# Hyena gate after duo attention on one core: the inverse transform of two batches split into a cosine and a sine part

## The chip, the core and the metric

The kernel runs on one core of a Trainium2 chip. The time is that of the device, in microseconds (us), from the first to the last instruction of one execution. PE is the matrix engine (TensorE), DVE the vector engine, ACT the scalar engine, POOL the GpSimd engine and SP the engine whose queue issues most of the DMAs.

## What is computed

Attention for 4 batches of 8 heads with 768 tokens of 64 numbers is followed by a gated long convolution. Four heads are causal over all keys ("R"); four see 4 sink tokens and a window of 64 ("L"). Cut to what matters here:

```python
a = softmax(where(mask, q @ k.T / 8, -1e9))      # per batch and head
x = (a @ v)                                      # put together to (4, 768, 512)
x1, x2, x3 = split(x @ w_proj, 3)                # 512 -> 3 * 512
X2 = rfft(x2, n=768, axis=1)
H  = rfft(filter_fft, n=768, axis=0)
conv = irfft(X2 * H, n=768, axis=1)
out = (x1 * conv * x3) @ w_out
```

The inverse transform `irfft` of the last two of the four batches is what changes.

## The kernel before

The work is a list of some 990 small named operations. The string `FAST` fixes in which order they are written, and with that the order on every engine: `name/engine@slot`, where `/v`, `/s`, `/p` and `/d` put an operation on DVE, ACT, POOL or a DMA of SP, and the slot is one of four places of two PSUM banks. A matmul group whose slot still holds an unread result waits for the reader. No scheduler changes this order afterwards.

Attention runs over n = 0 to 15, which are pairs of heads (batch n // 4). Pair n has `cqk` (cast of q and k), `T` (transposes them, from n = 8 by DMA on SP's queue), `sc` (scores, PE), `ex` (exp, ACT), `mk` (mask, DVE), `at` (values, PE), `rec` and `nm` (normalise, DVE), `fd`, `fe`, `fA`, `fS`, `fb`, `fr` (folds ahead of the forward transform, DVE or POOL), `W` (forward transform over tokens, PE), and `tn` (transposed attention for the projection). `lv15` loads v of the last pair, and `cv15` casts it.

The gate runs over the batches b = 0 to 3:

- `X` (24 matmuls of 512 columns for each batch) projects the transformed tokens, `Xe` evicts the result, and `pa`, `pb`, `pc` multiply it with the filter's spectrum: the tile `P` with three thirds. `sw` swaps two halves of one third by DMA.
- `x1` and `x3` are the projections for the gate, in blocks cb = 0 to 3 of 128 channels and halves of 384 tokens; `xs` evicts `x1`, and `g` multiplies with `x3` from PSUM.
- `c{b}.{cb}.{r}` (L1190) is the inverse transform. The 768 tokens are two halves, token t and token t + 384. r = 0 and r = 1 are the sums over even and odd frequencies; each takes three matmuls of 384 columns, with a third of `P` as the weights and a tile of the table `Gi` as the moving operand. `ce` (fp32 copy to `evs`, which lies in the tile `angle`) and `cv{b}.{cb}.0` and `.1` (L1201, DVE, sum and difference, written to `conv`, which lies in `turns`) turn the two into the two halves.
- `y` multiplies `conv` into the gate (for cb = 3: with `x1s`, and `g` then comes last), and `o{b}.{i}.{part}` (L1225) is the output projection of 128 tokens: part 0 takes the blocks cb = 0 to 2, part 1 the block cb = 3. `oe` evicts and `st` stores. For b = 3 tile i = 5 is done in two halves of 256 columns (L1220).

At the end of the program b = 3 is alone with what is left of b = 2: its `c`, `cv`, `y` and `g` end in `o3.*`, the evictions and the stores.

The lines that the prediction's steps touch most are these:

```python
SPECTRUM = (((0, 0), (0, 1)), ((1, 0), (1, 1)), ((0, 2), (1, 2)))
INVERSE = (((1, 0, 3), (1, 1, 4), (2, 1, 5)), ((0, 0, 0), (0, 1, 1), (2, 0, 2)))
```

An entry of `INVERSE` names a third of `P`, its half and a tile of `Gi`: r = 0 needs the second third and one half of the last, r = 1 the first third and the other half of the last. Tiles 3 and 0 are cosines, 4 and 1 sines, and 5 and 2 hold cosines in rows 0 to 63 and sines in rows 64 to 127.

## Time and profile before

| what | value |
|---|---|
| time, median of 3 runs (lowest to highest) | 185.48 us (185.42 to 185.55) |
| profiled execution: span, its only time on record | 186.0 us |
| mean granted TensorE clock | 0.993 |
| matmuls of L1190 (inverse transform, all batches) | 96 of 384 columns |
| DMA | 33.44 MB, mean 180 GB/s |

The span lies 0.5 us above the median of the runs. A row of the profile's timeline gives the start and the length of a group of instructions, then engine, line, operation, output and input tiles, shapes and count. Matmuls overlap in the records, so the length of one matmul (0.33 us for 384 columns) is longer than the distance from one to the next; a row of x12 matmuls in the chain of work gives that distance when it is divided by 12.

### The profile page before, as it was taken

The numbers are of one execution on the slowest core, as the hardware profiler recorded it, in microseconds if no ns is written. First come the engines' busy times: TensorE is split into PE (matmuls) and PEld (weight loads), VectorE is DVE, ScalarE is ACT, GpSimd is POOL, SyncE is SP. The second block draws the span as 40 slices with busy tenths as digits, with TensorE's granted clock in tenths as the row PEclk, the third lists the DMA queues.
The fourth block names the chain that finished last, engine by engine and source line by source line (L and its number), as shares of the span: only waits on it lengthen the run. The fifth ranks groups of instructions, "written<-read, shape, count | busy, mean of one in ns | idle before, by whom it ended". The sixth has DMA issues, their size and how long they took to land.

```text
span 186.0 us, 4370 instructions
## 1 busy us (share of the span) xinstructions
PE 171.6 (92%) x1685; PEld 102.2 (55%) x1702; DVE 152.5 (82%) x297; ACT 142.2 (76%) x186; POOL 83.5 (45%) x99
## 2 busy tenths in 40 slices
...
GB/s 163 305 305 194 257 272 244 260 215 130 211 224 217 104 217 222 177 149 221 216 239 201 223 203 171 127 252 222 124 102 40 118 0 131 40 4 113 188 281 108
DMA packets 76836, 33.44 MB, mean 180 GB/s; under 512 B 66058, under 2 KB 73226, under 8 KB 76810
## 3 DMA queue, kind: packets, MB, share of 16 engines
...
q8 instruction: 14, 0.23, 0.6%
...
q14 instruction: 12, 0.10, 0.1%
...
## 4 chain that ended last, share of the span: by engine, by line
PE 65%; DMA 16%; ACT 4%; DVE 4%; SPq 3%; POOL 3%; issue 2%; POOLq 0%
PE f_x_ps L1160 20%; PE f_out_ps L1225 10%; PE f_X_ps L1125 10%; DMA f_filt<-in_moe_filter_fft_dram 7%; PE f_c_ps L1190 7%; PE f_sc L961 6%; PE f_att L1021 4%; DMA f_qkT<-f_qk_bf 4%; DMA f_v_f<-in_v_dram 3%; SPq L898 3%; DMA qk_ahead<-in_q_dram 2%; PE f_xt_ps L1094 2%; PE f_F_ps L768 1%; POOL f_fo L544 1%; PE f_W_ps L1082 1%
## 5 line engine op out<-in xcount | busy, mean ns | idle before, releaser
L978 ACT ACTIVATE f_pT<-f_sc 128x1024 bf16<-128x1024 f32 (+2 forms) x68 | 58.3, 914 | 4.1 <-PE f_sc L972 2.1
L1160 PE MATMUL f_x_ps<-f_xT,f_wproj 128*128 128x384 bf16 x256 | 48.4, 326 | 0.1
L1160 PEld LDWEIGHTS <-f_wproj 128*128 128x128 bf16 x256 | 23.5, 98 | 15.6 <-issue 0.4
L961 PE MATMUL f_sc<-f_qkT 64*128 64x128 bf16 (+3 forms) x328 | 21.1, 242 | 2.2 <-ACT f_pT L978 0.8
L1125 PE MATMUL f_X_ps<-f_wproj,f_xh 128*128 128x512 bf16 x91 | 22.1, 379 | 0.3
L1225 PE MATMUL f_out_ps<-f_wout,f_gy 128*128 128x512 bf16 x85 | 22.0, 379 | 0.3
L544 POOL TENSOR_TENSOR f_gy<-turns,f_gy 128x768 bf16<-128x768 bf16 x7 | 11.6, 1669 | 20.8 <-DVE f_gy L1179 11.3
L1190 PE MATMUL f_c_ps<-f_Gi,f_P 128*128 128x384 bf16 x96 | 18.7, 326 | 0.1
L1021 PEld LDWEIGHTS <-f_pT 128*128 128x128 bf16 x472 | 16.4, 97 | 4.0 <-issue 1.5
L541 ACT COPY f_o<-f_out_ps 128x1024 f32<-128x1024 f32 (+2 forms) x15 | 11.5, 788 | 8.8 <-PE f_out_ps L1225 8.8
L961 PEld LDWEIGHTS <-f_qkT 64*128 64x128 bf16 x328 | 11.1, 94 | 12.6 <-issue 8.4
L1201 DVE TENSOR_TENSOR turns<-angle,f_c_ps 128x384 bf16<-128x384 f32 x32 | 16.4, 547 | 1.7 <-ACT angle L541 1.3
L1021 PE MATMUL f_att<-f_v_aug,f_pT 128*128 128x65 bf16 x392 | 17.3, 193 | 0.4 <-DVE f_attn L1038 0.4
L544 POOL TENSOR_TENSOR f_fo<-f_attn 128x384 bf16<-128x384 bf16 x11 | 10.9, 1003 | 14.6 <-PE f_W_ps L1082 12.2
L1038 DVE TENSOR_TENSOR f_attn<-f_att,f_recs 128x768 bf16<-128x768 f32 x16 | 15.3, 954 | 0.4
L541 ACT CAST f_X<-f_X_ps 128x1024 bf16<-128x1024 f32 x11 | 11.1, 1016 | 5.9 <-PE f_X_ps L1125 5.9
L544 POOL TENSOR_TENSOR f_br<-f_fo,f_uv 128x256 bf16<-128x256 bf16 x9 | 6.9, 766 | 18.7 <-DVE f_uv L544 9.1
L1125 PEld LDWEIGHTS <-f_xh 128*128 128x128 bf16 x96 | 8.9, 98 | 10.5 <-issue 1.0
L537 POOL CAST f_qk_bf<-qk_ahead 128x768 bf16<-128x768 f32 (+1 forms) x10 | 11.4, 1149 | 4.4 <-DMA qk_ahead<-in_k_dram 4.3
L1225 PEld LDWEIGHTS <-f_gy 128*128 128x128 bf16 x92 | 8.5, 98 | 8.8 <-issue 0.4
L541 ACT CAST f_xh<-f_W_ps 128x768 bf16<-128x768 f32 x12 | 9.5, 801 | 4.6 <-PE f_W_ps L1078 4.6
L1190 PEld LDWEIGHTS <-f_P 128*128 128x128 bf16 x96 | 9.1, 98 | 6.0
...
## 6 DMA issues: line engine op xcount, KB each, us to landing
...
```

What stands on the lines that cost most here:

```text
L537: nc.gpsimd.tensor_copy(out=out, in_=in_)
L541: nc.scalar.copy(out=out, in_=in_)
L544: (nc.gpsimd if now["engine"] == "p" else nc.vector).tensor_tensor(out, a, b, op)
L961: nc.tensor.matmul(sc[:, bank, col:col + 128 * cnt], lhsT=keys, rhs=qkT(n)[rows, 0, 128 * i:128 * (i + cnt)], start=(col == 0 or not biase ...
L978: nc.scalar.activation(out=pT(n)[:, c, :, 0:w], in_=held[f"sc.{n}.{c}"][:, :, 0:w], func=AF.Exp, scale=SCALE)
L1021: nc.tensor.matmul(att[:, hh, 65 * i:65 * i + 65], lhsT=pT(n)[:, c, bank, col:col + 128], rhs=values, start=(z == 0), stop=(z == len(here) ...
L1038: nc.vector.tensor_mul(attn(n).rearrange("p i hh d -> p hh i d"), rows[:, :, :, 0:64], recs()[:, n][:, :, :, None].to_broadcast([128, 2, N ...
L1125: nc.tensor.matmul(ps[:, u, :], lhsT=xh(b)[:, cc, chain, 128 * part:128 * part + 128], rhs=wproj()[:, cc, DM:2 * DM], start=(cc == 0), sto ...
L1160: nc.tensor.matmul(ps[:, s, 0:HS], lhsT=wproj()[:, cc, part * DM + cb * 128:part * DM + (cb + 1) * 128], rhs=xT(b)[:, cc, s * HS:s * HS + HS],
L1190: nc.tensor.matmul(ps[:, r, 0:HS], lhsT=P(b)[:, t, u, ch], rhs=Gi()[:, tile_no], start=(m == 0), stop=(m == 2))
L1201: fn(conv[:, half * HS:half * HS + HS], held[f"evs.{b}.{cb}"], held[f"c_ps.{b}.{cb}"][:, 1, 0:HS])
L1225: nc.tensor.matmul(ps[:, i % 2, :], lhsT=gy(b)[:, cb, i * 128:(i + 1) * 128], rhs=wout()[:, cb, :], start=(cb == 0), stop=(cb == NC - 1))
```

## The change

For b = 2 and 3 (`MIRRORED`) the cosine part and the sine part of the inverse transform are kept apart, for 194 tokens (`MW`) of each half. The first two matmuls of a group then have 194 columns, one writing the cosine part and one the sine part of the same PSUM bank, and the third has 388 columns of a new table `Gp`, in which the rows 0 to 63 of tiles 2 and 5 stand in the first 194 columns and rows 64 to 127 in the last 194, with zeros elsewhere. `Gp` is made once (`Gp0` to `Gp4`, POOL: two memsets and three copies). `ce` and `cv` work on 388 columns and `cv` writes to a new tile `parts`. Then `cd` adds cosine and sine part for tokens 0 to 193 of both halves, and `cm` subtracts them, read backwards and with the halves exchanged, for tokens 194 to 383. `Gp` and `parts` lie in the three buffers of v's loads (`v_f32`); `angle` becomes 8 numbers longer to hold the wider `evs`.

From the spectrum of batch 2 on (`X2`) `FAST` has a new order, and 32 operations have another engine: among them on DVE instead of POOL `pa2.0`, `pb2.1`, `pa3.2`, `pb3.1`, `y3.1`, `y3.2`; on POOL instead of DVE `y1.2`, `y2.0` and the folds `fS` and `fA` of pairs 12, 13 and 15 and `fS14`; on ACT instead of DVE `ce1.2`, `ce3.2`, `ce3.3`, `cv15`, `We14`, `xs3.1`; on ACT instead of POOL `cv14`. Of the 16 new `cd` and `cm`, ten are on DVE and six on POOL. Ahead of `X2` only the names of slots 1 and 2 are exchanged.

The inverse transform of batch 3, block 3 on PE before (tile names with their numbers; `f_P_3` is the product of the spectra, `f_Gi` the table), r = 1:

```order
L1190 LDWEIGHTS f_P_3_2695
L1190 MATMUL f_c_ps_3_3_2807<-f_Gi_252,f_P_3_2695 128x384
L1190 LDWEIGHTS f_P_3_2695
L1190 MATMUL f_c_ps_3_3_2807<-f_Gi_252,f_P_3_2695 128x384
L1190 LDWEIGHTS f_P_3_2695
L1190 MATMUL f_c_ps_3_3_2807<-f_Gi_252,f_P_3_2695 128x384
```

The same group on PE after the change:

```order
L1226 LDWEIGHTS f_P_3_2709
L1226 MATMUL f_c_ps_3_3_2818<-f_Gi_252,f_P_3_2709 128x194
L1226 LDWEIGHTS f_P_3_2709
L1226 MATMUL f_c_ps_3_3_2818<-f_Gi_252,f_P_3_2709 128x194
L1226 LDWEIGHTS f_P_3_2709
L1226 MATMUL f_c_ps_3_3_2818<-f_Gp_2129,f_P_3_2709 128x388
```

The three matmuls stay three, and their columns go from 1152 to 776.

DVE ahead of the last gate product of batch 3 before (`f_c_ps_3_2` and `_3_3` are `cv` and `ce` of blocks 2 and 3, `turns<-turns,f_x1s` is `y3.3`, the last row `g3.3`):

```order
L1179 TENSOR_TENSOR f_gy_3_2641<-f_x1s_3_1_2764,f_x3_ps_3_1_2783 128x768
L535 COPY angle_87<-f_c_ps_3_2_2778 128x384
L1201 TENSOR_TENSOR turns_86<-angle_87,f_c_ps_3_2_2778 128x384 x2
L535 COPY angle_87<-f_c_ps_3_3_2807 128x384
L1201 TENSOR_TENSOR turns_86<-angle_87,f_c_ps_3_3_2807 128x384 x2
L544 TENSOR_TENSOR turns_86<-turns_86,f_x1s_3_3_2751 128x768
L661 TENSOR_SCALAR other_64<-f_rows_right_2842,differ_63 1x1
L1183 TENSOR_TENSOR f_gy_3_2641<-turns_86,f_x3_ps_3_3_2845 128x768
```

The same place on DVE after the change, from `g3.1` to `g3.3` (`2x190` is a `cm`, `2x194` a `cd`, `f_gy<-turns,f_gy` are `y3.1` and then `y3.2`):

```order
L1211 TENSOR_TENSOR f_gy_3_2670<-f_x1s_3_1_2741,f_x3_ps_3_1_2800 128x768
L1244 TENSOR_TENSOR f_parts_3_2_2847<-angle_87,f_c_ps_3_2_2805 128x388 x2
L550 TENSOR_TENSOR f_gy_3_2670<-turns_86,f_gy_3_2670 128x768
L1244 TENSOR_TENSOR f_parts_3_3_2858<-angle_87,f_c_ps_3_3_2818 128x388 x2
L550 TENSOR_TENSOR turns_86<-f_parts_3_2_2847 128x2x190
L550 TENSOR_TENSOR turns_86<-f_parts_3_3_2858 128x2x194
L550 TENSOR_TENSOR turns_86<-f_parts_3_3_2858 128x2x190
L550 TENSOR_TENSOR turns_86<-turns_86,f_x1s_3_3_2747 128x768
L550 TENSOR_TENSOR f_gy_3_2670<-turns_86,f_gy_3_2670 128x768
L1215 TENSOR_TENSOR f_gy_3_2670<-turns_86,f_x3_ps_3_3_2860 128x768
```

Two copies have gone to ACT, three new differences and sums and the products `y3.1` and `y3.2` have come. POOL has at the same time `cm3.0`, `cm3.1`, `cd3.1` and `cd3.2` in place of `y3.1` and `y3.2`.

SP's queue at the transposes of pairs 13 to 15 before (`f_qkT_15` is `T15`, `f_v_f32_15` is `lv15`, `f_xT_3` from `f_attn_12` is `tn12`, `out_0_dram` a store, `f_Xw_2` is `sw`):

```order
L933 DMA_TRANSPOSE f_qkT_13_2090<-f_qk_bf_13_2058 128x12x128
L933 DMA_TRANSPOSE f_qkT_14_2098<-f_qk_bf_14_2085 128x12x128
L898 DMA f_v_f32_15_2151<-in_v_dram 128x6x64 x2
L1265 DMA out_0_dram<-f_o_0_2_1828 128x2x512
L933 DMA_TRANSPOSE f_qkT_15_2166<-f_qk_bf_15_2087 128x12x128
L1103 DMA_TRANSPOSE f_xT_3_2247<-f_attn_12_2234 128x6x128
```

The same place of SP's queue after the change:

```order
L965 DMA_TRANSPOSE f_qkT_13_2090<-f_qk_bf_13_2058 128x12x128
L965 DMA_TRANSPOSE f_qkT_14_2111<-f_qk_bf_14_2085 128x12x128
L965 DMA_TRANSPOSE f_qkT_15_2121<-f_qk_bf_15_2087 128x12x128
L1323 DMA out_0_dram<-f_o_0_1_1434 128x2x512
L1323 DMA out_0_dram<-f_o_0_2_1828 128x2x512
L930 DMA f_v_f32_15_2294<-in_v_dram 128x6x64 x2
```

`T15` has moved ahead of a load and a store, and the load of v for pair 15 behind two stores. `tn12` came right behind `T15`; now it comes seven rows behind it, after `sw` and a store of batch 1.

The diff; of the table only its end is shown, since the rows above show what it moves:

```diff
@@ -54,6 +54,7 @@
 BLANKS = (2, 3, 2)
 SPLIT = (1, 2)
 COPIED = ()
+MIRRORED = (2, 3)
 APART = ()
 
 OPENING = """
@@ -61,66 +62,67 @@
 FAST = """
...
-oe3.5/s o3.2.0@0 oe3.0/s o3.2.1 o3.3.0@3 oe3.2/s o3.3.1 st3.1/v st3.5/v o3.4.0@1 oe3.3/s o3.4.1 oe3.4/s st3.0/v
-st3.2/v st3.3/v st3.4/v o3.5.1@2 oe3.6/s st3.6/s
...
+st3.0/v o3.2.1 o3.3.0@0 oe3.5/v gd3@2 o3.3.1 st3.1/v o3.4.0@1 o3.4.1 oe3.2/s oe3.3/s oe3.4/s st3.5/v gd4 st3.2/v
+st3.3/v st3.4/v
 """
@@ -362,7 +364,8 @@
     pre["identity"] = pool.tile([128, 128], BF16, name="identity")
     pre["mtab"] = pool.tile([128, 6, 128], BF16, name="mtab")
     pre["turns"] = pool.tile([128, 3, HS], I32, name="turns")
-    pre["angle"] = pool.tile([128, 3, HS], FP32, name="angle")
+    pre["flat"] = pool.tile([128, 3 * HS + 8], FP32, name="angle")
+    pre["angle"] = pre["flat"][:, 0:3 * HS].rearrange("p (m t) -> p m t", m=3)
 
     blank, table, fcol, tcol, par, tfrac, quarter, identity, mtab, turns, angle = (
         (lambda name=name: pre[name]) for name in (
@@ -514,7 +517,10 @@
             return fn
         return put
 
-    shared = {"x1s0": pre["angle"][:, 2].bitcast(BF16).rearrange("p (s t) -> p s t", s=2), "evs0": pre["angle"][:, 0], "evs1": pre["angle"][:, 1],
+    MW = HS // 2 + 2
+    flat = pre["flat"]
+    shared = {"x1s0": flat[:, 4 * MW:4 * MW + HS].bitcast(BF16).rearrange("p (s t) -> p s t", s=2),
+              "evs0": flat[:, 0:2 * MW], "evs1": flat[:, 2 * MW:4 * MW],
               "conv0": pre["turns"][:, 0].bitcast(BF16), "conv1": pre["turns"][:, 1].bitcast(BF16)}
 
     def buf(name, shape, dtype, tag=None):
@@ -734,6 +740,32 @@
             ev(Gi()[:, tiles[0]:tiles[-1] + 1].rearrange("p (u t) m f -> p u (t m f)", u=rows),
                held[f"Gi_ps{part}"][:, 0:rows, 0:2 * HS])
 
+    def Gp():
+        return buf("Gp", [128, 2, 2 * MW], BF16, "v_f321")
+
+    def last_tiles(lo, hi, u):
+        return Gi()[lo:hi, 2:6:3][:, u].rearrange("p u m f -> p u (m f)")[:, :, 0:MW]
+
+    @op("Gp0")
+    def _():
+        (nc.gpsimd if now["engine"] == "p" else nc.vector).memset(Gp().rearrange("p u t -> p (u t)"), 0.0)
+
+    @op("Gp1")
+    def _():
+        ev(Gp()[0:64, :, 0:MW], last_tiles(0, 64, slice(0, 2)))
+
+    @op("Gp2")
+    def _():
+        ev(Gp()[64:128, :, MW:2 * MW], last_tiles(64, 128, slice(0, 2)))
+
+    @op("Gp3")
+    def _():
+        ev(Gp()[64:65, 1, 0:MW], Gi()[64:65, 5].rearrange("p m f -> p (m f)")[:, 0:MW])
+
+    @op("Gp4")
+    def _():
+        (nc.gpsimd if now["engine"] == "p" else nc.vector).memset(Gp()[64:65, 1, MW:2 * MW], 0.0)
+
     @op("lfilt")
     def _():
         nc.gpsimd.dma_start(out=filt(), in_=moe_filter_fft.rearrange("(t p) c -> p t c", p=128))
@@ -1187,18 +1219,44 @@
                 def _(b=b, cb=cb, r=r, ch=ch):
                     ps = banks(f"c_ps.{b}.{cb}")
                     for m, (t, u, tile_no) in enumerate(INVERSE[r]):
-                        nc.tensor.matmul(ps[:, r, 0:HS], lhsT=P(b)[:, t, u, ch], rhs=Gi()[:, tile_no],
-                                         start=(m == 0), stop=(m == 2))
+                        lhsT, rhs, to = P(b)[:, t, u, ch], Gi()[:, tile_no].rearrange("p m f -> p (m f)"), slice(0, HS)
+                        if b in MIRRORED:
+                            to = (slice(0, MW), slice(MW, 2 * MW), slice(0, 2 * MW))[m]
+                            rhs = rhs[:, 0:MW] if m < 2 else Gp()[:, 1 - r]
+                        nc.tensor.matmul(ps[:, r, to], lhsT=lhsT, rhs=rhs, start=(m == 0), stop=(m == 2),
+                                         skip_group_check=True)
+
+            width = 2 * MW if b in MIRRORED else HS
 
             @op(f"ce{b}.{cb}")
-            def _(b=b, cb=cb):
-                ev(buf(f"evs.{b}.{cb}", [128, HS], FP32, f"evs{cb % 2}"), held[f"c_ps.{b}.{cb}"][:, 0, 0:HS])
+            def _(b=b, cb=cb, width=width):
+                buf(f"evs.{b}.{cb}", [128, 2 * MW], FP32, f"evs{cb % 2}")
+                ev(held[f"evs.{b}.{cb}"][:, 0:width], held[f"c_ps.{b}.{cb}"][:, 0, 0:width])
 
             for half, fn in ((0, nc.vector.tensor_add), (1, nc.vector.tensor_sub)):
                 @op(f"cv{b}.{cb}.{half}")
-                def _(b=b, cb=cb, half=half, fn=fn):
+                def _(b=b, cb=cb, half=half, fn=fn, width=width):
+                    if b in MIRRORED:
+                        to = buf(f"parts.{b}.{cb}", [128, 2, 2, MW], BF16, ("v_f322", "v_f320")[cb % 2])
+                        to = to[:, half].rearrange("p w t -> p (w t)")
+                    else:
+                        to = buf(f"conv.{b}.{cb}", [128, S], BF16, f"conv{cb % 2}")[:, half * HS:half * HS + HS]
+                    fn(to, held[f"evs.{b}.{cb}"][:, 0:width], held[f"c_ps.{b}.{cb}"][:, 1, 0:width])
+
+            if b in MIRRORED:
+                @op(f"cd{b}.{cb}")
+                def _(b=b, cb=cb):
+                    parts = held[f"parts.{b}.{cb}"]
                     conv = buf(f"conv.{b}.{cb}", [128, S], BF16, f"conv{cb % 2}")
-                    fn(conv[:, half * HS:half * HS + HS], held[f"evs.{b}.{cb}"], held[f"c_ps.{b}.{cb}"][:, 1, 0:HS])
+                    two(conv.rearrange("p (s t) -> p s t", s=2)[:, :, 0:MW], parts[:, :, 0], parts[:, :, 1], ALU.add)
+
+                @op(f"cm{b}.{cb}")
+                def _(b=b, cb=cb):
+                    parts = held[f"parts.{b}.{cb}"]
+                    conv = buf(f"conv.{b}.{cb}", [128, S], BF16, f"conv{cb % 2}")
+                    back = HS - MW
+                    two(conv.rearrange("p (s t) -> p s t", s=2)[:, ::-1, MW:HS], parts[:, :, 0, back:0:-1],
+                        parts[:, :, 1, back:0:-1], ALU.subtract)
 
             @op(f"y{b}.{cb}")
             def _(b=b, cb=cb):
```

More of the change, by code (lines that the diff above doesn't have):

```diff
@@ L119 @@
[L119 to L123 removed]
+angle2 angle1 turns1 turns2 wrap0 ones1 wrap2 blank2@0 ck0/p T0.1@1 wrap1 cq0/s blank0@2 ck1/p sin1 T0.0 size blank1@3
@@ new lines @@
+o0.5.0 mk11.0 o0.4.1 cv11/s te8/v o0.5.1 fr8 X1.0.1@3 rec10 nm10/v vx11/s fS9/p te9/s sc12.4@0 sc12.2@1 fA9/p oe0.5/s
+X1.0.0 pb1.2/v fe10/v mk11.2 ex12.4 x31.2.0@2 x31.2.1 fd10/v sc12.5@0 fr9 mk11.1 vs11/d Xe1.0/s at11.0@3 at11.1
+pc1.2/v ex12.2 ex12.5 tn10@1 g1.2 rec11 fb9/p W8.0@2 nm11/v W8.1 te10/s lk13 x11.1.1@0 tn11@1 x11.1.0 We8/s lv12
+pb1.0/v pa1.0/p te11/v x31.1.1@3 lq13 pb1.1/v sc12.3@2 cv13/s pc1.0/v xs1.1/s lk14 sc12.1@1 ex12.3 fe11/p pc1.1/v lv14
+sc12.0@0 fS10/v ex12.0 x31.1.0 c1.1.1@2 lq14 c1.1.0 g1.1 fd11/v mk12.2 fA10/v W9.0@0 x12.0.0@3 ex12.1 ce1.1/s W9.1
```

111 lines of the change are left out of this document (53 added, 58 removed).

## The prediction

> **What bounds the kernel now.** I read the busy shares first, then the busy time by stage from the spectrum of batch 2 on, because everything ahead of it keeps its order.
>
> ```profile
> PE 171.6 (92%) x1685; PEld 102.2 (55%) x1702; DVE 152.5 (82%) x297; ACT 142.2 (76%) x186; POOL 83.5 (45%) x99
> ```
>
> ```profile
> 116.90:137.00 20.10, 19.30 (x200) 10.65 (x201) 17.98 (x34) 16.94 (x23) 9.93 (x7) 1.00 0.79 182
> 137.00:152.00 15.00, 15.00 (x151) 10.44 (x151) 14.08 (x33) 9.01 (x14) 5.80 (x7) 1.00 0.23 62
> 152.00:158.30 6.30, 6.25 (x32) 3.05 (x32) 1.85 (x3) 2.07 (x3) 4.37 (x3) 1.00 0.36 109
> 158.30:165.00 6.70, 6.65 (x40) 3.82 (x39) 5.94 (x9) 2.51 (x3) 1.43 (x1) 1.00 0.05 19
> 165.00:175.40 10.40, 10.35 (x59) 5.57 (x58) 8.33 (x17) 3.80 (x5) 3.24 (x2) 1.00 0.26 99
> 175.40:180.60 5.20, 5.15 (x28) 2.54 (x26) 0.95 (x1) 3.01 (x6) 0.00 (x0) 1.00 0.69 263
> ```
>
> The columns are the stretch, its length, and the busy time of PE, weight loads, DVE, ACT and POOL; then the granted clock. PE is busy for all but 0.8 us of the first stretch and for practically all of the rest, at full clock: here a matmul that is left out is time that is left out, as long as nothing else becomes late. DVE is next (14.08 of 15.00 in the second stretch), with room between 152.0 and 158.3. The chain of waits says the same:
>
> ```profile
> 122.45 6.53 DMA f_qkT<-f_qk_bf
> 129.03 0.56 PE f_sc L961 x14
> ...
> 157.47 0.86 PE f_X_ps L1125 x4
> 158.34 2.60 PE f_x_ps L1160 x16
> ...
> 165.75 1.95 PE f_c_ps L1190 x12
> ...
> 180.21 0.86 ACT f_o L541 x2
> ```
>
> It is a DMA transpose until 129.03 and PE without a break from there to the last eviction at 180.21. The only wait of PE of any size is in the first stretch:
>
> ```profile
> PE f_sc L961 <- DMA f_qkT<-f_qk_bf: 0.6, 1, 0.6
> ```
>
> **What the matmuls save.** Distances from one matmul to the next give their price.
>
> ```profile
> 143.05 0.10 PEld L1074 LDWEIGHTS <-f_br 128*128 128x128 bf16 x1
> 143.21 0.27 PE L1074 MATMUL f_W_ps<-f_G,f_br 128*128 128x256 bf16 x1
> 143.32 0.27 PE L1076 MATMUL f_W_ps<-f_Gk,f_uv 128*128 128x256 bf16 x1
> 143.43 0.22 PE L1078 MATMUL f_W_ps<-f_G,f_br 128*128 128x128 bf16 x1
> 143.49 0.81 PE L1160 MATMUL f_x_ps<-f_xT,f_wproj 128*128 128x384 bf16 x4
> ```
>
> 256 columns take 0.11 us (143.21 to 143.32), 128 take 0.06, and 384 take 1.95 / 12 = 0.1625 by the chain. On the line between these, 194 columns take 0.085 and 388 take 0.164. A group goes from 3 x 0.1625 = 0.488 to 2 x 0.085 + 0.164 = 0.334, so it saves 0.154 us; 2 batches x 4 blocks x 2 groups make 16, **2.47 us**. The bounds: if a matmul with its own weight load could not come below the 0.10 us that a load lasts, the saving is 2.0; but 0.06 for 128 columns, with a load of its own, speaks against it.
>
> **What the transpose of pair 15 saves.** It is late because of SP's queue:
>
> ```profile
> 118.72 1.44 SPq L933 DMA_TRANSPOSE f_qkT<-f_qk_bf  x1
> 120.27 1.48 SPq L898 DMA_DIRECT2D f_v_f<-in_v_dram  x2
> 121.79 0.54 SPq L1265 DMA_DIRECT2D out_dram<-f_o  x1
> 122.45 3.63 SPq L933 DMA_TRANSPOSE f_qkT<-f_qk_bf  x1
> ```
>
> The four stand back to back, and the second transpose starts 2.2 us earlier if the load and the store are taken from between. It then lands some 2 us ahead of 129.0, and PE's wait of 0.6 us goes. I take **0.6 us**; the bounds are 0 (the transfers collide on the DMA engines, which are 0.79 busy there) and 0.8, the whole idle time of the stretch. What is moved back in the queue, the load of v for pair 15 and the transposed attention of pair 12, is read only by the values of pair 15 and the projections of batch 3, which PE reaches behind the output projection of batch 1 and the first `c2`; that work hides it, so I cost it at nothing. Without that cover PE would wait for as much as they are late.
>
> **What is added, by engine.** `Gp` (two memsets, three copies) and the moved casts go to POOL and ACT, which have 10 and 3 us idle in the first stretch; nothing there is priced. Every `cd` and `cm` is a sum of two bf16 tensors of 388 or 380 numbers, and these rows stand nearest:
>
> ```profile
> L544 DVE TENSOR_TENSOR f_fo<-f_attn 128x384 bf16<-128x384 bf16 x21 | 8.6, 423 | 0.0
> 127.46 0.61 DVE L544 TENSOR_TENSOR f_fo<-f_attn 128x384 bf16<-128x384 bf16 x2
> L1201 DVE TENSOR_TENSOR turns<-angle,f_c_ps 128x384 bf16<-128x384 f32 x32 | 16.4, 547 | 1.7 <-ACT angle L541 1.3
> 171.43 1.02 DVE L1201 TENSOR_TENSOR turns<-angle,f_c_ps 128x384 bf16<-128x384 f32 x2
> L544 POOL TENSOR_TENSOR f_fo<-f_attn 128x384 bf16<-128x384 bf16 x11 | 10.9, 1003 | 14.6 <-PE f_W_ps L1082 12.2
> ```
>
> Two in a row on DVE last 0.61, so each takes about 0.3 of its queue (the mean of 423 ns has stretched ones in it); with PSUM and fp32 (the `cv`) two last 1.02, or 0.5. No row reads backwards. `cm` lies between 0.3 (as `f_fo`) and 0.5 (as `cv`) on DVE, and on POOL from 1.0 upwards; I take 0.3 and 1.0, for the shape is that of `f_fo`. The Trainium skill (VectorE: DVE Perf Modes, What auto-detection checks) lets 16-bit operands run two at a time at a step of plus or minus one; by that `cm` costs what `cd` does, by the slow end three `cm` behind each other cost 0.6 us more. No run here shows a step of minus one.
>
> Batch 2 has cover: six of its eight `cd` and `cm` are on DVE ahead of the multiplications of batch 3, and the last of them fall where 152.0 to 158.3 was, in which DVE is busy for 1.85 of 6.30. Without that room each would put off the next `P` by 0.3. PE's new order has 9 projection groups between that spectrum and the first `c3`, which covers the multiplications of `P`, now all on DVE.
>
> **The place that decides is batch 3's last blocks.** Count from the end of its `X` matmuls (158.33 before). PE has, up to the first `o3`, 13 projection groups of 4 matmuls (2.60 / 4 = 0.65), six `o2` of 4 with 512 columns (0.86, as the `X` row of the chain) and 8 `c3` (0.334): 8.45 + 5.2 + 2.7 = **16.3 us**. DVE has in the same time, each started when its input is there:
>
> ```profile
> 163.03 1.29 DVE L544 TENSOR_TENSOR f_P<-f_P,f_m 128x1024 bf16<-128x1024 bf16 x2
> 169.51 0.55 DVE L544 TENSOR_TENSOR f_gy<-turns,f_gy 128x768 bf16<-128x768 bf16 x1
> 169.97 0.95 DVE L1179 TENSOR_TENSOR f_gy<-f_x1s,f_x_ps 128x768 bf16<-128x768 bf16 x1
> ```
>
> The last `pc` ends at 6.9 (0.6 for each of eight, from the eviction of the last `X` at 1.1, with `y2.3` and `g2.3` between); `g3.2` (0.9) at 7.7; `cv3.0` starts when PE ends `c3.0.1` at 8.3 and ends at 9.3; `cd3.0`, `cv3.1` to 10.6; `y3.0` (0.46 to the next start), `g3.1` to 11.9; `cv3.2` to 12.9; `y3.1` at 12.8, behind `cm3.1` and `cd3.1` on POOL (10.7 + 2 x 1.0); `cv3.3` to 14.3; `cm3.2`, `cd3.3`, `cm3.3` to 15.1; `y3.3`, `y3.2` to **16.2**. The first `o3` needs `y3.2`: 16.2 against 16.3. So the new chain fits with nothing to spare, and each tenth that DVE is slower PE waits. Before, DVE had 8.33 of 10.40 there.
>
> What makes DVE slower is POOL beside it:
>
> ```profile
> 147.35 1.63 POOL L544 TENSOR_TENSOR f_br<-f_fo,f_uv 128x256 bf16<-128x256 bf16 x2 [1.75 <-PE f_c_ps L1190]
> 147.57 0.88 DVE L1066 SCALAR_TENSOR_TENSOR f_br<-f_uv,f_fo 128x256 bf16<-128x256 bf16 x1
> 149.31 0.41 DVE L1066 SCALAR_TENSOR_TENSOR f_br<-f_uv,f_fo 128x256 bf16<-128x256 bf16 x1
> ```
>
> The same operation takes 0.88 beside POOL and 0.41 alone. Not each one is hit, but `cd3.0`, `y3.0` and `y3.1` now run beside `cm` and `cd` on POOL. The Trainium skill (GPSIMD Engine Reference, Specifications) has the two engines share SBUF interfaces, with contention for DVE instructions that have two SBUF inputs; the trace agrees with its 0.88 against 0.41, and the rule speaks against this change, which puts such pairs side by side at the tightest place. Three hits of 0 to 0.47 are 0 to 1.4 us; I take **0.5 us** of new wait, and 0.2 (0 to 0.4) for PSUM slots in the first stretch, whose readers stand on ACT behind the casts that it gets.
>
> **The end.** After the last matmul there is an eviction and a store, as before:
>
> ```profile
> 180.01 0.60 PE L1220 MATMUL f_out_ps<-f_wout,f_gy 128*128 128x256 bf16 x4
> 181.10 0.38 ACTq L1243 DMA_DIRECT2D out_dram<-f_o  x1
> ```
>
> Now the last piece is 128x512 from SP in place of 128x256 from ACT: an eviction longer by 0.2, one less of the two evictions in a row (0.86). I cost it at 0, from -0.4 to +0.4.
>
> **The sum** against the profiled span: 186.0 - 2.47 - 0.6 + 0.5 + 0.2 = 183.4. The span is 0.5 above the median of the runs, so I forecast 185.48 - 2.4 = **183.1 us**.
>
> **The rivals.**
>
> 1. The tail takes most of it. `cm` at 0.5, and contention at the upper end, make `y3.2` late by 0.6 + 1.4 instead of 0.5: 183.1 + 1.5 = 184.6. For it: the slack of 0.1. Against: the eight `cv` there read PSUM, and the row of the `cv` shows no stretching (mean 547 ns of 32, POOL busy or not). Between this and the forecast lies everything from 183.6 to 185.2.
> 2. Slower than before: `cm` on POOL is far dearer backwards than forwards. POOL has `cm3.0`, `cm3.1` and `cd3.1` in a row ahead of `y3.1`, behind which all the rest of DVE's queue stands. With p for a backward `cm` on POOL, `y3.2` ends at about 9.4 + 2p + 1.0 + 3.4 = 13.8 + 2p, so PE waits 2p - 2.5. Above p = 2.7 us this eats what is left of the 3.1 us won; at 3.2 it is 3.9, and the time 185.48 - 3.07 + 0.2 + 3.9 = 186.5. For it: no row reads backwards on POOL. Against: POOL's rows go by the number of elements (1.63 / 2 = 0.8 for 256, 1.0 for 384), and both directions touch as many.
> 3. The change does not do what it says: narrow matmuls are held at the weight load's 0.10, the saving is 2.0, and the time 183.6. Against it stand the 0.06 us above.
>
> **Chances.** The forecast's own case (182.2 to 183.6; at the low end 2.47 + 0.8 are won and nothing new waits) 0.60; the third rival, with its time at the upper edge of this, 0.05; the first 0.27, of which 0.04 ends within 0.2% of before; the second 0.08, of which 0.01 does so. 0.2% is about what a measurement of this kernel can tell from no change. So faster 0.88, same 0.05, slower 0.07. The range goes from 182.0, below which only a shorter end could lead, to 184.9: it leaves out the slow rival and the upper part of the first.
>
> **What would show it.** Right: L1226 with some 0.33 us for each group; no wait of PE for the transpose near 128; the last `X` of batch 3 ending near 156, and the first `o3` some 16.3 to 17.3 us later; a wait of PE for DVE or POOL of 0.3 to 1.0 us there. `cm` on DVE at 0.3 like `cd`, on POOL at 1.0. Wrong: `cm` rows far above `cd` rows; waits of PE for slots or for POOL between 120 and 150; an end later than 5.4 us after the last matmul (186.0 - 180.6).

## The result and the profile after

| | before | changed |
|---|---|---|
| time, median of 6 runs each (lowest to highest) | 186.06 us (185.42 to 187.38) | 184.22 us (183.27 to 185.29) |
| ratio to before, 95% interval | | 0.9888 [0.9838, 0.9937] |
| profiled execution, span | 186.0 us | 183.0 us |
| start of the first `X2` matmul | 116.77 | 115.77 |
| from there to the end of the last matmul | 63.84 us | 60.62 us |
| from the end of the last matmul to the end | 5.40 us | 6.62 us |

The change makes the kernel faster by some 1.1%, about 2 us. The changed kernel was timed twice more beside the experiments: ratios 0.9836 [0.9796, 0.9876] and 0.9853 [0.9808, 0.9898]. The time of an execution lies about 1.6 us above its span (the profiled one of the changed kernel took 184.64 us for a span of 183.0), so the profiled execution of before, with a span of 186.0, was one of its longer ones; the text above set that span only 0.5 us above a median.

The first thing to see is that the total is too coarse. Ahead of `X2` the two programs are the same but for two slot names, and yet `X2` starts 1.0 us sooner; in 14 profiles of both kernels and of the experiments that start lay between 114.1 and 117.2 us, without a pattern. From it to the last matmul, however, the changed kernel took 60.62 us in each of three profiles. So the stages are compared, and the start is left out.

PE's rows at both ends of the stretch, of before (its last row stands in the prediction) and of the changed kernel; start, length, engine, line and operation:

```profile
116.77 0.81 PE L1125 MATMUL f_X_ps<-f_wproj,f_xh 128*128 128x512 bf16 x2
```

```profile
115.77 0.81 PE L1157 MATMUL f_X_ps<-f_wproj,f_xh 128*128 128x512 bf16 x2
...
175.14 1.25 PE L1283 MATMUL f_out_ps<-f_wout,f_gy 128*128 128x512 bf16 x5
```

The busy time by stage (to the start of the last `X` matmul of batch 3, to the end of the last projection ahead of `o3`, to the last matmul; columns as in the prediction), before and then after:

```profile
116.77:157.96 41.19, 40.34 (x380) 24.04 (x381) 34.04 (x68) 28.14 (x38) 19.89 (x17) 1.00 0.52 125
157.96:175.42 17.46, 17.36 (x98) 9.58 (x99) 14.27 (x25) 6.31 (x8) 5.01 (x3) 1.00 0.19 74
```

```profile
115.77:154.35 38.58, 38.26 (x376) 23.49 (x378) 32.25 (x66) 30.06 (x40) 22.63 (x27) 1.00 0.47 119
154.35:171.00 16.65, 16.54 (x101) 9.72 (x102) 15.82 (x30) 8.35 (x11) 3.96 (x4) 1.00 0.31 105
171.00:176.39 5.39, 5.39 (x30) 2.53 (x27) 2.58 (x6) 2.13 (x4) 0.00 (x0) 1.00 0.74 276
```

PE is still busy throughout, at full clock. Part of the idle time in these rows (0.85 and 0.32 us in the first stage) is missing records: of 507 matmuls from `X2` on, seven have none in the profile of before and six in that of the changed kernel, and each leaves a gap of 0.05 to 0.16 us. The second and third profile of the changed kernel have all 507, and no gap between two of them. DVE, in the second stage, has gone from 14.27 of 17.46 to 15.82 of 16.65: it is as full as the prediction feared. Yet PE's waits from there on are one line, and no engine is in it:

```profile
PE f_X_ps L1157 <- issue: 0.2, 1, 0.2
```

This one is the gap of a missing record (0.16 us).

The inverse transform on PE (three groups of three matmuls) and the new sums in the page's groups, where the two numbers behind the bar are busy time and mean ns of one:

```profile
162.63 0.99 PE f_c_ps L1226 x9
```

```profile
L550 POOL TENSOR_TENSOR turns<-f_parts 128x380 bf16<-128x380 bf16 x3 | 3.1, 1031 | 11.1 <-DVE f_parts L1244 11.0
L550 POOL TENSOR_TENSOR turns<-f_parts 128x388 bf16<-128x388 bf16 x3 | 2.7, 915 | 2.2 <-DVE f_gy L550 1.8 <-DVE f_parts L1244 0.4
L550 DVE TENSOR_TENSOR turns<-f_parts 128x388 bf16<-128x388 bf16 x5 | 1.8, 359 | 0.8 <-POOL f_gy L550 0.7
L550 DVE TENSOR_TENSOR turns<-f_parts 128x380 bf16<-128x380 bf16 x5 | 1.8, 353 | 0.0
```

A group takes 0.99 / 3 = 0.33 us. `cm` (380 numbers, read backwards) takes DVE 353 ns and `cd` (388, forwards) 359.

The end of the program in the waits of SP's queue (line 1357 before and 1415 after are the closing code), before and then after:

```profile
SPq L1357 <- DMA out_dram<-f_o: 1.6, 2, 1.3
SPq L1357 <- PEq L1357: 0.7, 2, 0.5
```

```profile
SPq L1415 <- PEq L1415: 1.7, 2, 1.1
SPq L1415 <- DMA out_dram<-f_o: 1.5, 1, 1.5
```

SP waits for the last store about as long as before, and then a microsecond more for another engine's sequencer. The view names PE's, which had long been done; the records of the sequencers show that GpSimd came last. How that is, the experiments below tell.

### The profile page after: what moved, and what is told of

Its sections match the earlier page's. It is cut to its first block, busy times and chain, and to the rows that moved or that the text cites. A ratio compares the mean times of both kernels' runs of the same rounds, so it can differ in the third digit from the quotient of the medians.

```text
span 183.0 us, 4399 instructions
## 1 busy us (share of the span) xinstructions
PE 168.8 (92%) x1686; PEld 102.3 (56%) x1702; DVE 153.4 (84%) x303; ACT 145.6 (80%) x189; POOL 85.4 (47%) x111
## 4 chain that ended last, share of the span: by engine, by line
PE 73%; DVE 7%; DMA 6%; ACT 5%; issue 2%; POOL 2%; SPq 1%; POOLq 0%
PE f_x_ps L1192 22%; PE f_X_ps L1157 11%; PE f_out_ps L1283 11%; PE f_sc L993 8%; DMA qk_ahead<-in_q_dram 6%; PE f_att L1053 6%; PE f_c_ps L1226 5%; PE f_xt_ps L1126 2%; ACT f_pT L1010 2%; DVE angle L682 1%; PE f_qkT_ps L955 1%; POOL f_fo L550 1%; PE f_W_ps L1114 1%; PE f_W_ps L1108 1%; PE f_W_ps L1106 1%
## 5 line engine op out<-in xcount | busy, mean ns | idle before, releaser
L1192 PE MATMUL f_x_ps<-f_xT,f_wproj 128*128 128x384 bf16 x256 | 47.3, 326 | 0.0
L550 POOL TENSOR_TENSOR f_uv<-f_fo 128x256 bf16<-128x256 bf16 x15 | 11.0, 747 | 15.5 <-DVE f_fo L550 15.4
L1053 PEld LDWEIGHTS <-f_pT 128*128 128x128 bf16 x472 | 16.3, 97 | 2.6 <-issue 0.9
L547 ACT COPY f_o<-f_out_ps 128x1024 f32<-128x1024 f32 (+2 forms) x13 | 10.8, 832 | 5.4 <-PE f_out_ps L1283 5.4
L1226 PE MATMUL f_c_ps<-f_Gi,f_P 128*128 128x384 bf16 (+1 forms) x80 | 14.5, 294 | 0.0
L550 POOL TENSOR_TENSOR f_fo<-f_attn 128x384 bf16<-128x384 bf16 x10 | 10.0, 1009 | 9.4 <-PE f_W_ps L1114 7.5
L547 ACT CAST f_xh<-f_W_ps 128x768 bf16<-128x768 f32 x13 | 10.3, 801 | 3.9 <-PE f_W_ps L1110 3.8
L550 POOL TENSOR_TENSOR turns<-f_parts 128x388 bf16<-128x388 bf16 (+1 forms) x6 | 5.8, 973 | 13.3 <-DVE f_parts L1244 11.4
L1028 DVE TENSOR_TENSOR f_pT<-f_pT,mtab 128x1024 bf16<-128x1024 bf16 (+1 forms) x18 | 11.8, 664 | 0.0
```

The costliest lines, as they stand in the source:

```text
L547: nc.scalar.copy(out=out, in_=in_)
L550: (nc.gpsimd if now["engine"] == "p" else nc.vector).tensor_tensor(out, a, b, op)
L1028: nc.vector.tensor_mul(some, some, tab.to_broadcast([128, 2, cols, 128]))
L1053: nc.tensor.matmul(att[:, hh, 65 * i:65 * i + 65], lhsT=pT(n)[:, c, bank, col:col + 128], rhs=values, start=(z == 0), stop=(z == len(here) ...
L1192: nc.tensor.matmul(ps[:, s, 0:HS], lhsT=wproj()[:, cc, part * DM + cb * 128:part * DM + (cb + 1) * 128], rhs=xT(b)[:, cc, s * HS:s * HS + HS],
L1226: nc.tensor.matmul(ps[:, r, to], lhsT=lhsT, rhs=rhs, start=(m == 0), stop=(m == 2), skip_group_check=True)
```

## The experiments

All stages in one table; the last three columns count from the end of the last matmul. "GpSimd closed" is the end of its closing drain; "SP closed" is the start of SP's last drain, some 0.2 us after SP has seen the last store land. The "check" in the names of runs is `gd0` to `gd4`, five small steps that make the number on which every engine branches at the end.

| kernel | `X2` to last matmul | GpSimd closed | SP closed | end |
|---|---|---|---|---|
| before | 63.84 | -0.63 | 4.57 | 5.40 |
| changed | 60.62 | 5.78 | 4.83 | 6.62 |
| changed, second and third profile | 60.62, 60.62 | 5.57, 5.62 | 4.64, 4.67 | 6.42, 6.47 |
| new order, old transform | 63.13 | 5.74 | 4.83 | 6.59 |
| old order, new transform | 67.62 | -0.13 | 5.17 | 6.00 |
| batch 2 alone split | 61.87 | 5.79 | 4.92 | 6.64 |
| transpose of pair 15 back | 61.10 | 5.71 | 4.78 | 6.56 |
| POOL beside DVE | 62.51 | 5.67 | 4.72 | 6.51 |
| 4 sums more on DVE | 61.95 | 5.75 | 4.81 | 6.60 |
| 2 sums more on POOL | 62.77 | 5.59 | 4.66 | 6.44 |
| changed, check early (two profiles) | 60.63, 60.62 | 1.24, 1.40 | 4.58, 5.01 | 5.41, 5.84 |
| before, check late | 63.89 | 4.36 | 5.31 | 6.13 |

The expectations that were written first have 60.47 and 63.52 us for the stretches of 60.62 and 63.84, read from rows that were grouped otherwise.

**The changed kernel again.**

> The changed kernel once more, unaltered, on the chip of the runs beside it. It measures how far a second profile repeats the first: from the first matmul of X2 to the last matmul 60.47 us, from there to the end 6.6 us. If the 1.0 us by which the whole changed stretch already starts earlier than before comes from the run and not from the change, the start of X2 (115.9 in the first profile) may move by up to 1 us here; the stretch itself should repeat within 0.2. Ratio to the kernel before 0.984 to 0.994.

`X2` started at 114.38, 1.4 us sooner than in the first profile; the stretch took 60.62 us again. So the start moves from run to run by itself, and a difference of 0.1 us in the stretch can be read from one profile.

**The new order without the new transform.**

```diff
-MIRRORED = (2, 3)
+MIRRORED = ()
...
-cd2.1/v cm2.1/v cd2.0/v cm2.0/v ... cd3.3/v cm3.3/v
```

> The changed kernel's new order with the old inverse transform for all batches: no cosine and sine parts, so Gp, cd and cm are left out and every c has three matmuls of 384 columns. Theory (the narrower matmuls bring 2.47 us, the earlier transpose of pair 15 brings 0.6): X2 to last matmul 60.5 + 2.5 = 62.9 to 63.0 us, against 63.52 before; DVE lighter, so no new wait. Rival (the new order does most of it, and narrower matmuls are hidden behind the chain of DVE): 60.5 to 61.5 us. The end stays at 6.6 us by the theory of the late check, since the check stands where the change put it.

63.13 us: in this order some `y` read `conv` after the next block was written there, which changes the output and not the work. The rows of the `c` are at their old price (three groups):

```profile
164.95 1.46 PE f_c_ps L1204 x9
```

So the narrower matmuls bring 63.13 - 60.62 = 2.51 us, and the order 63.84 - 63.13 = 0.71. The median was 186.64 us, ratio 1.0006 [0.9968, 1.0044]: the order alone wins 0.7 us in the stretch and gives 1.2 back at the end. The rival (the order does it all) falls.

**Batch 2 alone.**

```diff
-MIRRORED = (2, 3)
+MIRRORED = (2,)
...
-cm3.0/p ... cd3.0/v ... cm3.1/p ... cd3.1/p ... cd3.2/p ... cm3.2/v cd3.3/v cm3.3/v
```

> The changed kernel with the split transform for batch 2 alone; batch 3 has its three matmuls of 384 columns back and neither cd nor cm. Theory (the saving is that of the matmuls, 8 groups x 0.157 us for each batch, and no engine beside PE takes any of it): 60.62 + 1.25 = 61.87 us from X2 to the last matmul, all of the difference behind the last X of batch 3 (22.04 + 1.25 = 23.29); end 6.5. Rival (the chain of DVE in batch 3 has taken part of that batch's saving): less than 61.7, since that chain is shorter without cd3 and cm3.

61.87 us, as expected to the digit: 8 groups x 0.157 for each batch, all of it behind the last `X` of batch 3. The chain of DVE takes nothing of batch 3's saving.

**The transpose back in its place.**

```diff
-X2.1.1 T14 cv1.3.1 cv14/s x31.3.0@0 cv1.2.1 T15 vx14/p st0.3 ... st0.5 ... lv15
+X2.1.1 T14 lv15 st0.5 T15 st0.3 cv1.3.1 cv14/s x31.3.0@0 cv1.2.1 vx14/p
```

> The changed kernel with the transpose of pair 15 put back in SP's queue behind the load of v for pair 15 and one store, as before. Theory (its earlier place is worth 0.6 to 0.7 us): a wait of PE for f_qkT of 0.5 to 0.7 us comes back in the first stretch, and X2 to last matmul grows from 60.62 to 61.1 to 61.3 us. Rival (the new order of PE reads that transpose later anyway, and the 0.7 us come from elsewhere in the order): 60.6, no such wait.

61.10 us, so the earlier place is worth 0.48 us. The wait is back in PE's waits, and SP's queue shows the cause as before: the third transpose behind a load and a store.

```profile
PE f_sc L993 <- DMA f_qkT<-f_qk_bf: 0.3, 1, 0.3
```

```profile
114.61 3.65 SPq L965 DMA_TRANSPOSE f_qkT<-f_qk_bf  x2
118.36 1.50 SPq L930 DMA_DIRECT2D f_v_f<-in_v_dram  x2
119.91 0.54 SPq L1323 DMA_DIRECT2D out_dram<-f_o  x1
120.57 2.78 SPq L965 DMA_TRANSPOSE f_qkT<-f_qk_bf  x1
```

The view's 0.3 is less than the 0.48, since it counts from the end of a record, and records overlap. From start to start the two matmuls around this wait are 0.51 us apart, and 0.05 without a wait, so it costs 0.46. The other 0.23 of the order's 0.71 us lie in the same wait: the transpose landed 12.21 us behind the start of `X2` in the kernel before and 11.98 in this run, 0.23 sooner, and PE started the scores 0.04 later in both. From there to the last matmul PE needs the same in both, within 0.01: 51.58 us before, and here 49.08 + 2.51 for the narrower matmuls. So this one wait accounts for all that the order brings.

**How much room DVE has.** Four sums whose result nothing reads stand ahead of `y3.2`:

```diff
-cd3.3/v cm3.3/v y3.3/v y3.2/v
+cd3.3/v cm3.3/v y3.3/v jk1/v jk2/v jk3/v jk4/v y3.2/v
...
+    two(junk()[:, 0], junk()[:, 0], junk()[:, 1], ALU.add)
```

> The changed kernel with four idle sums of 384 bf16 numbers on DVE directly ahead of y3.2 (some 0.3 us each, 1.2 together); nothing reads their result. It measures how much room DVE has in batch 3's last blocks, which the prediction put at 0.1 us. Theory (room of 0.1 to 0.2 us, as the changed kernel's rows show: y3.2 ends 0.2 ahead of the third o3 matmul that reads it): PE waits 1.0 to 1.1 us for f_gy, and X2 to last matmul grows from 60.62 to 61.6 to 61.7 us. Rival (DVE has more room, which is why no wait was seen): growth below 0.6 us.

61.95 us. The added sums took more than expected, 171.30 - 169.85 = 1.45 us, and PE waits:

```profile
169.85 1.53 DVE L550 TENSOR_TENSOR f_junk<-f_junk 128x384 bf16<-128x384 bf16 x4
171.30 0.55 DVE L550 TENSOR_TENSOR f_gy<-turns,f_gy 128x768 bf16<-128x768 bf16 x1
```

```profile
PE f_out_ps L1295 <- DVE f_gy L550: 1.1, 1, 1.1
```

Counted from start to start this wait costs 1.31 us (1.53 less the usual 0.22 of a matmul of 512 columns).

The stretch grew by 1.33, so DVE's room in the changed kernel is 1.45 - 1.33 = 0.12 us. The prediction said 0.1.

**POOL beside DVE.** Three such sums on POOL, behind `cd3.2`:

```diff
-cd3.2/p y3.1/v
+cd3.2/p jk1/p jk2/p jk3/p y3.1/v
```

> The changed kernel with three idle sums of 384 bf16 numbers on POOL behind cd3.2 (and a memset before), so that POOL runs beside cm3.2, cd3.3, cm3.3, y3.3, y3.2 and g3.3 on DVE; nothing reads their result. Theory of the prediction (a DVE sum of two bf16 tensors of SBUF beside POOL stretches from 0.41 to 0.88 us at times): these rows stretch by 0.1 to 0.5 each, y3.2 ends 0.5 to 1.4 later, and PE waits for DVE at the first o3 by 0.3 to 1.2; X2 to last matmul 60.9 to 61.8. Rival (no contention; the 0.88 had another cause): rows unchanged at 0.3 to 0.55, stretch 60.62 within 0.1.

62.51 us, above the range of the theory (60.9 to 61.8) and far from its rival. The three sums `cm3.2`, `cd3.3`, `cm3.3` on DVE, which take 0.89 in the changed kernel, take 2.90 as long as POOL runs; the two products behind them are as ever:

```profile
167.68 2.90 DVE L550 TENSOR_TENSOR turns<-f_parts 128x380 bf16<-128x380 bf16 x3
170.61 0.56 DVE L550 TENSOR_TENSOR turns<-turns,f_x1s 128x768 bf16<-128x768 bf16 x1
171.09 0.55 DVE L550 TENSOR_TENSOR f_gy<-turns,f_gy 128x768 bf16<-128x768 bf16 x1
```

```profile
167.47 2.88 POOL L550 TENSOR_TENSOR f_junk<-f_junk 128x384 bf16<-128x384 bf16 x3
```

2.01 us later less the room of 0.12 makes the 1.89 by which the stretch grew. Taken one by one, the three end 0.21, 0.22 and 0.22 us after the POOL sum that ran when they started (alone each takes 0.35): they do not share, they are held until it is done. The Trainium skill (SBUF — State Buffer, Who interferes with whom) calls the ports that the two engines share an exclusive lock, lets a DVE instruction with two SBUF inputs contend with a GpSimd one that reads SBUF, and says that the order of issue decides who blocks; these rows agree.

That is also why the changed kernel pays nothing. Its rows at that place, DVE and then POOL:

```profile
164.23 0.37 DVE L550 TENSOR_TENSOR turns<-f_parts 128x388 bf16<-128x388 bf16 x1
164.51 1.02 DVE L1244 TENSOR_TENSOR f_parts<-angle,f_c_ps 128x388 bf16<-128x388 f32 x2
165.44 0.55 DVE L550 TENSOR_TENSOR f_gy<-turns,f_gy 128x768 bf16<-128x768 bf16 x1
165.91 0.95 DVE L1211 TENSOR_TENSOR f_gy<-f_x1s,f_x_ps 128x768 bf16<-128x768 bf16 x1
166.78 1.02 DVE L1244 TENSOR_TENSOR f_parts<-angle,f_c_ps 128x388 bf16<-128x388 f32 x2
167.72 0.55 DVE L550 TENSOR_TENSOR f_gy<-turns,f_gy 128x768 bf16<-128x768 bf16 x1
168.18 1.02 DVE L1244 TENSOR_TENSOR f_parts<-angle,f_c_ps 128x388 bf16<-128x388 f32 x2
169.12 0.89 DVE L550 TENSOR_TENSOR turns<-f_parts 128x380 bf16<-128x380 bf16 x3
170.05 0.56 DVE L550 TENSOR_TENSOR turns<-turns,f_x1s 128x768 bf16<-128x768 bf16 x1
170.52 0.55 DVE L550 TENSOR_TENSOR f_gy<-turns,f_gy 128x768 bf16<-128x768 bf16 x1
```

```profile
164.27 1.01 POOL L550 TENSOR_TENSOR turns<-f_parts 128x380 bf16<-128x380 bf16 x1 [10.70 <-DVE f_parts L1244]
165.61 1.87 POOL L550 TENSOR_TENSOR turns<-f_parts 128x380 bf16<-128x380 bf16 x2 [0.33 <-DVE f_parts L1244]
167.88 1.08 POOL L550 TENSOR_TENSOR turns<-f_parts 128x388 bf16<-128x388 bf16 x1 [0.40 <-DVE f_parts L1244]
```

Each DVE sum of two SBUF tensors starts just ahead of POOL's (164.23 against 164.27, 165.44 against 165.61, 167.72 against 167.88) or after it has ended (169.12 against 168.96), and what runs on DVE during POOL's sums reads PSUM (L1244 and L1211, at their usual 1.02 and 0.95). POOL is the one that waits, and it has time. The order gives this, not chance alone: each of the three POOL sums behind a pause is released by the end of a `cv` on DVE (in brackets), and DVE goes on to its own next sum 0.04 to 0.17 us before POOL starts, by the same margins within 0.01 in all three profiles of the changed kernel.

**A dearer POOL.** Two such sums on POOL ahead of `cd3.1`:

```diff
-cm3.1/p cv3.2.1 cd3.1/p
+cm3.1/p cv3.2.1 jk1/p jk2/p cd3.1/p
```

> The changed kernel with two idle sums of 384 bf16 numbers on POOL ahead of cd3.1 (some 1.0 us each); nothing reads their result. It stands for a dearer cm on POOL, the prediction's second rival, whose formula gives a wait of PE of 2p - 2.5 us with p the price of one of two cm; two more microseconds are p = 2.0, so 1.5 us. Theory (the formula holds, y3.1 holds up DVE's queue): X2 to last matmul 60.62 + 1.5 = 62.1 us, within 0.3, with DVE waiting for POOL at y3.1. Rival (DVE and PE have other room, POOL's delay is swallowed): growth below 0.8 us.

62.77 us: 2.15 more, where the formula of the second rival says 1.5. The rows of POOL, and then of DVE:

```profile
168.09 1.89 POOL L550 TENSOR_TENSOR f_junk<-f_junk 128x384 bf16<-128x384 bf16 x2
169.93 1.63 POOL L550 TENSOR_TENSOR turns<-f_parts 128x388 bf16<-128x388 bf16 x2
```

```profile
170.80 1.17 DVE L550 TENSOR_TENSOR f_gy<-turns,f_gy 128x768 bf16<-128x768 bf16 x1 [1.57 <-POOL turns L550]
```

DVE waits 1.57 us for `cd3.1`, as the formula has it, and then `y3.1` takes 1.17 instead of 0.55: `cd3.2` on POOL has started in the meantime (at 170.72, the second half of the row at 169.93). So this delay on POOL came with a second price, 0.62 us, which the formula lacks.

**The new transform in the old order.** `Gp` is made behind `pa2.0`, and each `cd` and `cm` stands on DVE behind its `cv`:

```diff
-pa2.0/p X2.2.0@3 ... cv2.1.0 c2.0.0@1 cv2.1.1 fA13/v
+pa2.0/p Gp0/p Gp1/p Gp2/p Gp3/p Gp4/p X2.2.0@3 ... cv2.1.0 c2.0.0@1 cv2.1.1 cd2.1/v cm2.1/v fA13/v
```

> The split transform in the order of before: Gp0 to Gp4 on POOL behind pa2.0, and cd, cm on DVE directly behind each pair of cv. Theory (the split saves 2.47 us of matmuls, and the order is needed for the new DVE work, 0.6 to 0.7 us for each of 8 pairs): the transpose wait of 0.6 is back, PE waits for DVE in batch 3's last blocks, where cd3.x and cm3.x add 2.6 us to DVE: 63.52 - 2.47 + 0.5 to 1.5 = 61.5 to 62.5 us from X2 to the last matmul; end 5.5 us, since the check stands where it stood. Rival (DVE has room, the new order was not needed): 61.0 to 61.1. Rival (order carries the change): 63 or more, nothing won.

67.62 us, 3.8 slower than before: the theory and its first rival fall. The number is that of the second rival (63 or more, nothing won) but not its reason, since the order alone brings 0.71 us: the new transform is what needs it. The time agrees, with a median of 190.12 us and a ratio of 1.0178 [1.0114, 1.0243]. PE's waits are spread over the whole stretch, the largest for POOL and DVE:

```profile
PE f_W_ps L1110 <- POOL f_br L550: 0.8, 1, 0.8
PE f_out_ps L1283 <- DVE other L667: 0.6, 1, 0.6
PE f_c_ps L1226 <- DVE f_gy L1211: 0.6, 1, 0.6
PE f_out_ps L1283 <- DVE f_gy L1211: 0.6, 1, 0.6
```

The expectation counted only what `cd3` and `cm3` add to DVE at the end. But `Gp` (2.3 us on POOL) also stands ahead of a POOL product, which now runs where DVE starts a mask, and the mask lasted 2.62 us (the mean of its kind is 0.68 in the changed kernel), until 0.55 us after POOL's end:

```profile
124.35 2.66 POOL L550 TENSOR_TENSOR f_m<-f_X,f_HAB 128x1024 bf16<-128x1024 bf16 x1
```

```profile
124.94 2.62 DVE L1028 TENSOR_TENSOR f_pT<-f_pT,mtab 128x1024 bf16<-128x1024 bf16 x1
```

That is one place of several; what each of them costs was not taken apart. The new order brings 0.7 us for the old transform and 7.0 for the new one (67.62 - 60.62); the 7.0 belong to this placement of `Gp`, `cd` and `cm`, and no other placement in the old order was run.

**The check early.** `gd0` to `gd4` make the number (`other`) that GpSimd, like the other engines, reads before its last branch:

```diff
-gd0 pa3.2/v ... g3.2 gd1 st2.1 ... g3.3 o3.0.1 gd2 oe3.0/s ... gd3@2 o3.3.1 ... st3.5/v gd4 st3.2/v
+gd0 gd1 gd2 pa3.2/v ... cv3.3.0 gd3@0 x33.3.0@3 ... g3.3 gd4 o3.0.1
```

> The changed kernel with the four small steps of the sanity check (gd1 to gd4, which write the number on which GpSimd's last branch waits) moved ahead: gd1 and gd2 right behind gd0, gd3 ahead of x33.3.0, gd4 behind g3.3. Theory (the end is 1.05 us longer since GpSimd comes late to its branch, fetches its closing code after it and drains last): from last matmul to end 5.5 instead of 6.6 us, from the last store's landing to the end 1.1 instead of 2.05; X2 to last matmul unchanged at 60.5 within 0.2; total 1.0 us shorter, about 0.5% against the changed kernel. Rival (the last store of 512 columns from SP's queue in place of 256 from ACT sets the end): end stays at 6.6 us, total unchanged. Second rival: gd1 and gd2 (wide DVE operations) ahead of the spectrum of batch 3 delay it, and the stretch grows by up to 0.5 us.

The stretch is unchanged at 60.63, and the end is 5.41 us. The table shows the rule: in every row the end comes 0.82 to 0.85 us after the later of "GpSimd closed" and "SP closed". The nine profiles of the new order with the late check have GpSimd later by 0.87 to 0.95 us. SP's waits are again those of before:

```profile
SPq L1415 <- DMA out_dram<-f_o: 1.2, 2, 0.6
SPq L1415 <- PEq L1415: 0.7, 2, 0.5
```

The time, however, was 183.23 us against 183.15 for the unaltered kernel on the same chip, so both were timed again.

> The changed kernel once more, as the partner of the run beside it. X2 to last matmul 60.62 us, last matmul to end 6.4 to 6.6. The start of X2 has lain between 114.1 and 117.2 us in the profiles so far, whatever the kernel, so the median of the times may lie anywhere from 182.9 to 184.3.

> The changed kernel with gd1 to gd4 moved ahead, once more: its first timing lay 0.1 us from the unaltered kernel's although its profile ended 1.0 us sooner after the last matmul. Theory (the end is 1.0 us shorter in each execution, and the first timing drew later openings by chance): again 5.4 us from last matmul to end, and over both timings together the median 0.5 to 1.0 us below the unaltered kernel's. Rival (the gain is given back ahead of X2, because the moved steps shift the rest of the program): X2 starts a microsecond later than in the unaltered kernel's runs again, and the medians agree within 0.2.

183.31 us against 184.08, with ratios to before of 0.9793 [0.9745, 0.9842] and 0.9853 [0.9808, 0.9898], which is 1.1 us apart. In the profile the check is early again (1.40) but the last store landed later, so the end was 5.84. The rival's start of `X2` a microsecond later is not there (115.72 against 115.19). The end is better in both profiles, by 1.0 and 0.6 us; a gain in the total is likely, and the two timings together (0.1 us slower by the medians, then 0.8 faster; by the ratios 0.3 and 1.1 faster) do not prove its size, since the intervals overlap. By its ratios to before it is the fastest version that was run.

**The late check in the kernel before.**

```diff
-cv3.1.1 gd2 o2.5.1 ... o2.2.1 gd3@3 gd4 x33.3.0@0
+x33.3.1 g3.3 gd2 o3.0.0@2 ... gd3@2 o3.3.1 ... o3.4.0@1 gd4 oe3.3/s
```

> The kernel before, with the sanity check's last steps moved to where the change has them: gd2 behind g3.3, gd3 ahead of o3.3.1, gd4 behind o3.4.0. Theory (a late check alone costs the longer end): X2 to last matmul 63.84 us as before (within 0.2), last matmul to end 6.4 to 6.6 instead of 5.40. Rival (the longer end belongs to the new last store or to another order of the stores): 5.4.

6.13 us, and not for the reason given: GpSimd closed at 4.36, ahead of SP at 5.31, which had waited longer for its last store (2.3 us in its waits, 1.6 before). With the store as quick as in the profile of before, SP would close at 4.57, still after GpSimd. So, by this one profile, a late check alone costs the kernel before nothing. In its order a piece of the output projection stands behind `gd4`, so the branch comes 0.33 us after the last matmul and not 0.85, and from the branch to the closing drain are 3.23 us and not 3.9 to 4.1.

## Why the prediction was right, and where it was not

The time of 184.22 us lies in the range and the direction was right. It is 1.1 us above the forecast of 183.1, and 0.6 of that is the kernel before, whose median was 186.06 this time and not 185.48. The change itself, -2.4 forecast, came out at -1.8 by the medians and at -2.0 to -2.2 by the stages. That this is so near is luck: two errors nearly cancel. The prediction counted -2.37 us in the stretch and 0 at the end; measured are -3.22 in the stretch and +1.0 to +1.2 at the end. A slip stands in its sum too: 186.0 - 2.47 - 0.6 + 0.5 + 0.2 is 183.6 and not 183.4, but the forecast goes by the difference of 2.4, which is right.

- **Narrower matmuls, 2.47 us**: right. 0.33 us for each group, 2.51 by the order alone against the changed kernel, 1.25 of it for one batch. The third rival (matmuls held at their weight load, a saving of 2.0) falls by the same numbers.
- **Transpose of pair 15, 0.6 us**: right in kind, and 0.1 too small: it is the whole 0.71 of the order. The 0.6 is the idle time in the view of waits, which leaves out the overlap of the records; the transpose put back late in the new order cost 0.48, because it landed 0.23 us sooner than before.
- **The tail of batch 3**: the count was right. `y3.2` was to end 16.2 us behind the last `X` and the first `o3` to start at 16.3; the room was 0.1, and 0.12 was measured. That the room fits so well is in part chance: counted from the end of that `X`, `y3.2` ended at 16.35 and PE reached `o3` at 16.1, but only the third matmul of `o3`, which starts 0.43 later, waits for `y3.2`, as the run with four sums more on DVE shows. The step that failed is "Three hits of 0 to 0.47", with its 0.5 us: it took the row of 0.88 against 0.41 as a price that some sums pay at random. The runs show a condition in its place: a DVE sum of two SBUF tensors waits if a POOL sum is running when it starts, until that one ends, and pays nothing if it starts first. The pair of rows that the prediction read is a case of it: POOL started at 147.35, DVE at 147.57, and DVE's 0.88 us end 0.28 us after POOL's first product. None of the three sums is hit, for DVE starts first at each; so the wait of PE of 0.3 to 1.0 us, one of the signs of being right, is not there. With the condition met, the rival's case is real: 1.89 us in the run with POOL beside.
- **PSUM slots in the first stretch, 0.2 us**: not there; the profiles with all records have no gap on PE at all.
- **`cm` backwards**: right at `cd`'s price on DVE, 353 against 359 ns, and 1.0 to 1.1 us on POOL where 1.0 was taken. Each `cm` on POOL started while a DVE sum ran; a `cd` in that case takes 1.08 us as well, and 0.83 otherwise, so its price without a wait was not seen. The second rival's mechanism exists (two microseconds more on POOL cost 2.15), but its condition is not met.
- **The end, "I cost it at 0, from -0.4 to +0.4"**: failed, and it is the largest miss. The step looked at the last eviction and the last store, which take as long as before (SP closed 4.57 before, 4.64 to 4.83 after). It did not look at `gd2` to `gd4`, three steps of the new order with next to no share of the busy time, which now stand among and behind the last matmuls. GpSimd can branch only after them, needs 3.9 to 4.1 us from its branch to its closing drain, and so closes after the stores. An end later than 5.4 us was one of the prediction's signs of being wrong, and it came.

What stays open: where the 7.0 us of the old order go, one by one, and why the way from the branch to the drain is longer (2.6 to 3.0 us for early branches, 3.2 to 4.1 for late ones). The DMA records have fetches of instructions in that time, beside the last stores; that these hold GpSimd up is not shown.
